# A kernel of attention, two mixing layers and a gated convolution: q of the first head pair in zero-padded tiles, first-layer copies a slot later in the drain, a block's split moved into the value layer

## The chip, the cores and the metric

One core of a Trainium2 chip runs the whole program. The metric is the device time of one execution in microseconds; several executions are timed and their median is given. The engines are named PE (TensorE), DVE (VectorE), ACT (ScalarE), POOL (GpSimd) and SP (SyncE). Each takes its instructions in the order in which the program issues them; DMAs are issued from the queues of SP, ACT and POOL.

## The reference, cut to what matters

All inputs are float32 except the weights, which come as float64: batch 4, 8 heads, 576 rows, head size 64, so a model width of 512.

```python
scores = q @ k.T / sqrt(64)                       # per batch and head, 576 x 576
scores = where(scores >= max(scores) - tau, scores, -1e9)
attn = exp(scores - max(scores)); attn /= sum(attn) + 1e-9
x = attn @ v                                      # heads side by side: 4 x 576 x 512
u = x + (x.T @ U @ V).T                           # rank 32, over the rows
y = u + relu(u @ w_ch1) @ w_ch2                   # 512 -> 2048 -> 512
gate = sigmoid(sum(conv_w[k] * y shifted by 4 - k rows, k = 0..4))
out = (gate * (y @ w_val)) @ w_out
```

## The kernel before, in words

Every product of float32 matrices is done with numbers split in two: a high part, rounded by a copy to the fast matmul type, and a low part, the rest (number minus high part). A product is then three matmuls (high by high, high by low, low by high), four for the scores of pair 0. The high part is nearly always a copy on ACT, the low part a subtraction on DVE behind it.

**Attention** goes through 16 pairs of heads, nine tiles of 128 query rows for each pair. Each tile is a slot `s`: nine slots a pair, `NS` = 155 slots with the drain. A slot takes one tile through one step of each stage: `scores` on PE, `soft_max` (L412, DVE: negation and maximum), `soft_exp` (L426, exponential on ACT, and L427, the threshold `th` on POOL, which the mask needs), `soft_mask` (L437, DVE), transposes `trans_main` and `trans_tail` (L453, L470), then `pv` (L496, L507), `back`, `mix_t`, `mix_u` and `mix_ut` for the whole pair. The copies that follow a PE step are put down with `later(s + 1, k, fn, name)`: they are issued in slot `s + 1` in four batches `k`, each sorted by `LATE_ORDER`. PE's steps of a slot come after them, sorted by `ORDER`.

q and k of a pair are loaded by `load_qk` (L258, DMAs at L266 and L271), transposed by `prep_T` (L327, L335, L338) and split by `hi_lo_qk` (L306; L313 and L315 on ACT, L319 and L323 on DVE). From pair 1 on, `stacks` copies high and low parts with DMAs into tiles `st` of 128 rows, in which high and low part lie one above the other. Pair 0 has no stacks: `scores` takes 64 rows of `qk` for each head (L386, L398, and L391 where the columns are rotated). Tile 0 of each pair takes the last 64 rows of both heads from `bd`, which `tails` (L369, four POOL copies) fills. Setup order is L571 to L616; `warm` is a series of transposes of the identity, and the four batches of copies of pair 0 are issued behind it.

Loads of weights and their conversion from float64 (`from_f64`, L103 to L131) are generators that `work.tick()` moves on a step at a time.

**The drain.** From slot 144 on, no scores are left, and each slot also takes one step of `dense_front` (L780): it splits block 0 of u (512 columns; `split_block`, L749 on ACT, L750 on DVE), runs the first layer `h1` (L767) on blocks 0 and 1, one tile of 12 matmuls (`passes`, L765) and its two copies (L773, L774) a slot, and splits blocks 1 and 2.

**The dense layers** run over four chunks of the hidden width and five blocks of columns (four of 512, one of 256): `h1` and `ch` (L818, L826) in turn, so that one tile's copies lie beside the next one's matmuls. Behind them come the gates (`gate_step`: taps on ACT, L834; L849 on DVE; sigmoid, L841), the value layer `val` (L885: 12 matmuls, product with the gate L895 on DVE, high part L896 on ACT, low part L897 on DVE) and `proj` (L903, L911), whose tiles ACT copies (L915) and SP stores (L917). `val` of block n + 1 needs the split of y's block n + 1, which stood behind `val` of block n.

Of the kernel before, what the change touches and what calls it, by code (L numbers as in the profile page):

```python
# [36 lines left out]
def attention_moe_kernel(  # L37
# [188 lines left out]
    def attention(dense_front, dense_mid, dense_back):  # L226
# [31 lines left out]
        def load_qk(p):  # L258
            eng = nc.gpsimd if 1 < p < 4 else nc.sync
            b, h = divmod(2 * p, H)  # L260
# [3 lines left out]
            for nm, src, o in (("qn", q, "(t p) d -> p t d"), ("kn", k, "(p t) d -> p t d")):  # L264
                for hh in range(2):
                    eng.dma_start(  # L266
                        out=t[nm][:, :, hh * D:(hh + 1) * D], in_=src[b, h + hh, 0:SM, :].rearrange(o, p=128)
                    )
                    yield
# [56 lines left out]

        def prep_T(s, p, nm):  # L327
            d = st8[p]
            if nm == "q":
                d["qk"] = qk_p.tile([128, 4, S], F32R, tag="qk", name="qk")  # L330
            x = xtile("tm")
            parts = []
            if nm != "tail":
                for i in range(4):
                    nc.tensor.transpose(x[:, i * 128:(i + 1) * 128], d[nm + "n"][:, i, :], idn)  # L335
                parts.append(hi_lo_qk(p, nm, x, 0, SM))
            else:
                nc.tensor.transpose(x[:, 0:128], d.pop("tn"), idn)  # L338
                for m, nn in enumerate("qk"):
                    parts.append(hi_lo_qk(p, nn, x[:, m * TL:(m + 1) * TL], SM, TL))  # L340
# [31 lines left out]
        def scores(p, i):  # L372
# [5 lines left out]
            else:  # L378
# [6 lines left out]
                else:  # L385
                    z = d["qk"][hh * D:(hh + 1) * D]  # L386
                    ops = [(z[:, m, c:c + 128], z[:, n, :]) for m in (0, 3) for n in (1, 2)]
# [30 lines left out]
        def soft_exp(p, i):  # L418
# [8 lines left out]
            nc.gpsimd.tensor_tensor(out=th, in0=nm, in1=tau_eff, op=ALU.add)  # L427
# [142 lines left out]

        for p in range(2):  # L571
            for _ in load_qk(p):
                pass
        nc.scalar.dma_start(out=tau_sb, in_=tau.partition_broadcast(128))
        make_identity(nc, idn)
        nc.scalar.activation(out=ntau, in_=idn[:, 0:1], func=ACTF.Exp)
# [32 lines left out]
        for nm in ("q", "k", "tail"):  # L609
# [5 lines left out]
        tails(0)  # L615
# [52 lines left out]
        for s in range(NS):  # L668
# [39 lines left out]
            if s >= 9 * NP:  # L708
                next(dense_front, None)
                for _ in range(1): work.tick()  # L710
# [34 lines left out]
    def split_block(src, pool=None):  # L745
        t = (pool or p1["us"]).tile([128, 2, KD, NB], F32R, tag="us", name="us")
        for o, m, s in src:
            for e in range(0, KD, 2):
                nc.scalar.activation(out=t[:, 0, e:e + 2, o:o + m], in_=s[:, e:e + 2], func=ACTF.Copy)  # L749
                nc.vector.tensor_tensor(  # L750
                    out=t[:, 1, e:e + 2, o:o + m], in0=s[:, e:e + 2], in1=f(t[:, 0, e:e + 2, o:o + m]),
                    op=ALU.subtract,
                )
        return t
# [12 lines left out]
    def h1(c, us, n):  # L767
        m = size[n]
        t = p1["h"].tile([128, 2, KD, NB], F32R, tag="h", name="h")
        for e in range(KD):  # L770
            ps = p1["a"].tile([128, 512], F32, tag="a", name="a")
            passes(ps, w1[c % 2][0], us, e, m)
            nc.scalar.activation(out=t[:, 0, e, 0:m], in_=ps[:, 0:m], func=ACTF.Relu)  # L773
# [3 lines left out]
            yield t  # L777


    def dense_front():  # L780
# [4 lines left out]
        us = split_block(u_src(0), p1["us"])  # L785
        yield
# [3 lines left out]
        for t in h1(0, us, 0):  # L790
# [4 lines left out]
        for t in h1(0, us2, 1):  # L795
            yield
        p1["t"].append(t)
        yield
# [15 lines left out]
    def dense():  # L814
# [70 lines left out]
        def val(n, ys):  # L885
            t = p1["h"].tile([128, 2, KD, NB], F32R, tag="h", name="g")
            for e in range(KD):
# [4 lines left out]
                m = size[n]  # L892
                passes(ps, w1[NCH % 2][0], ys, e, m)
                g = u[:, e, n * NB:n * NB + m]
                nc.vector.tensor_tensor(out=g, in0=ps[:, 0:m], in1=g, op=ALU.mult)  # L895
                nc.scalar.activation(out=t[:, 0, e, 0:m], in_=g, func=ACTF.Copy)  # L896
                nc.vector.tensor_tensor(out=t[:, 1, e, 0:m], in0=g, in1=f(t[:, 0, e, 0:m]), op=ALU.subtract)  # L897
                tick()
            return t
# [3 lines left out]
        def proj(n, t):  # L903
            w = w2[NCH % 2][0]
            for g in range(size[n] // 128):
# [9 lines left out]
                nc.scalar.activation(out=o, in_=ps, func=ACTF.Copy)  # L915
                r0 = n * NB + g * 128
                nc.sync.dma_start(out=outf[r0:r0 + 128, :], in_=o)  # L917
# [30 lines left out]
        for n in range(NN):  # L948
            t = val(n, us)
            if n + 1 < NN:  # L950
                us = split_block(y_src(n + 1))
# [40 lines left out]
```

## Time and profile before

| | |
|---|---|
| median of 3 runs | 856.49 us |
| the runs | 854.17, 859.28, 856.49 us |
| the profiled execution's own time | 854.32 us |
| its span | 852.4 us |
| mean granted clock of PE | 0.994 |
| PE busy | 826.8 us, 97% of the span |
| DVE, ACT, POOL busy | 609.9, 438.2, 241.5 us |

The profiled execution is one more run than the three. Its span goes from the first to the last thing the profiler saw; 1.9 us of its time lie outside. A busy PE is not PE at its peak, since matmuls overlap; so the places where it waits and the clock that it was granted are read beside the share. The granted clock of 1.00 is 2.4 GHz, 0.50 is 1.2 GHz. In a timeline row, the bracket gives the idle time of the engine before the instruction and what ended it.

### The profile page before, as it was taken

Reading aid. Unit: us, or ns where it says so; the run is one execution under the profiler, and the core shown is the slowest. Engines: PE = TensorE matmul, PEld = TensorE weight load, DVE = VectorE, ACT = ScalarE, POOL = GpSimd, SP = SyncE. Lnnn points to the kernel's source line nnn. Section 1 sums busy time; section 2 is a strip of 40 time slices with the busy share of each in tenths; the row PEclk is TensorE's granted clock in tenths of the full one; section 3 lists DMA queues with packets and bytes.
Section 4 is the critical chain, followed back from the end, with each engine's and each line's share of the span. In section 5 each row is a group of like instructions: output and inputs, shape, how many; then the busy total and the mean of one; then the engine's idle time right before and its main releaser. Section 6 shows DMA issues by size and latency. Waiting matters only on the chain.

```text
span 852.4 us, 14266 instructions
## 1 busy us (share of the span) xinstructions
PE 826.8 (97%) x5084; PEld 695.1 (82%) x5084; DVE 609.9 (72%) x1293; ACT 438.2 (51%) x890; POOL 241.5 (28%) x342
## 2 busy tenths in 40 slices
PE   8999999999999999899999999999999999999998
PEld 7887887887887888678888888888888888878886
DVE  6689888888988987436784785347753588988850
ACT  4688888887887887422232333133322334345532
POOL 6756433632433422001341244003420143200000
PEclk9799999999999999999999999999999999999999
DMA  5665755765675541001220122002210111001111
GB/s 133 159 142 127 175 134 129 167 160 129 149 174 129 133 107 46 0 1 50 75 74 26 49 75 75 1 1 77 71 50 1 41 58 50 1 1 38 62 50 75
DMA packets 63423, 68.07 MB, mean 80 GB/s; under 512 B 43333, under 2 KB 46549, under 8 KB 63354
## 3 DMA queue, kind: packets, MB, share of 16 engines
q1 hardware_dynamic: 61786, 64.07, 29.3%
q0 software_dynamic: 1424, 3.10, 1.3%
q8 instruction: 41, 0.67, 0.3%
q14 instruction: 28, 0.23, 0.1%
q10 hardware_dynamic: 144, 0.00, 0.0%
HBM read 35.89 MB, written 4.72 MB: 48 GB/s over the span
## 4 chain that ended last, share of the span: by engine, by line
PE 75%; DVE 10%; ACT 6%; issue 2%; DMA 2%; POOL 2%; SPq 1%; ACTq 0%; POOLq 0%; DVEq 0%
PE a L765 23%; PE c L765 20%; PE o L507 7%; PE p L911 6%; PE s L398 5%; PE v L765 5%; PE xm L453 4%; DVE u L849 3%; PE t L546 2%; PE o L496 2%; DVE e L437 1%; ACT pt L462 1%; DMA qn<-in_q_dram 1%; ACT e L426 1%; ACT qk L313 1%
## 5 line engine op out<-in xcount | busy, mean ns | idle before, releaser
L765 PE MATMUL c<-h,w 128*128 128x512 f32 (+1 forms) x960 | 200.9, 368 | 1.3 <-ACT u L568 1.3
L765 PE MATMUL a<-us,w 128*128 128x512 f32 (+1 forms) x960 | 201.5, 368 | 0.0
L765 PEld LDWEIGHTS c<-h,w 128*128 128x128 f32 x960 | 167.3, 189 | 31.7 <-ACT u L568 1.7
L765 PEld LDWEIGHTS a<-us,w 128*128 128x128 f32 x960 | 167.2, 189 | 30.2 <-issue 0.4
L773 ACT ACTIVATE h<-a 128x512 fp32r<-128x512 f32 (+1 forms) x80 | 44.2, 554 | 196.9 <-PE a L765 196.7
L427 POOL TENSOR_TENSOR th<-nm,tau_eff 128x1 f32<-128x1 f32 x144 | 81.5, 566 | 182.7 <-DVE ns L412 181.2
L131 POOL TENSOR_TENSOR wf<-wf,wt 128x512 f32<-128x512 f32 (+2 forms) x43 | 57.2, 1330 | 257.2 <-DVE wt L126 257.2
L774 DVE SCALAR_TENSOR_TENSOR h<-a,h 128x512 fp32r<-128x512 f32 (+1 forms) x80 | 50.9, 637 | 108.1 <-ACT h L773 107.9
L412 DVE TENSOR_SCALAR_CACHE_REDUCE ns<-s 128x576 f32<-128x576 f32 x144 | 108.3, 752 | 26.3 <-PE s L398 25.8
L437 DVE SCALAR_TENSOR_TENSOR e<-ns,th,e 128x576 f32<-128x576 f32 x144 | 119.6, 831 | 6.7 <-POOL th L427 6.3
L426 ACT ACTIVATE e<-ns,nm 128x576 f32<-128x576 f32 x144 | 111.4, 773 | 23.1 <-DVE ns L412 22.7
L398 PE MATMUL s<-st 128*128 128x288 f32 x480 | 94.7, 319 | 2.6 <-DVE ns L412 2.4
L453 PE MATMUL xm<-idn,e 128*128 128x128 f32 x576 | 88.8, 278 | 7.2 <-DVE qk L323 6.0
L462 ACT ACTIVATE pt<-xm 128x512 f32<-128x512 f32 x144 | 85.1, 591 | 4.9 <-PE xm L453 2.4
L398 PEld LDWEIGHTS s<-st 128*128 128x128 f32 x480 | 68.2, 189 | 16.6 <-issue 7.7
L453 PEld LDWEIGHTS xm<-idn,e 128*128 128x128 f32 x576 | 69.8, 142 | 12.8 <-ACT pt L462 6.0
L507 PE MATMUL o<-pt,vt 128*64 128x256 f32 (+1 forms) x768 | 69.8, 331 | 0.0
L507 PEld LDWEIGHTS o<-pt,vt 128*64 128x64 f32 x768 | 41.4, 137 | 24.5 <-issue 8.0
L172 POOL TENSOR_TENSOR w<-wf,w 128x512 fp32r<-128x512 f32 x36 | 54.0, 1516 | 10.0 <-ACT w L170 10.0
L849 DVE SCALAR_TENSOR_TENSOR u<-y,cw,u 128x576 f32<-128x576 f32 x64 | 55.0, 873 | 0.6
L826 DVE TENSOR_TENSOR y<-c,y 128x64 f32<-128x64 f32 (+4 forms) x96 | 39.8, 448 | 21.2 <-PE c L765 21.2
L750 DVE TENSOR_TENSOR us<-u,us 128x1024 fp32r<-128x1024 f32 (+1 forms) x40 | 46.8, 1211 | 10.2 <-ACT us L749 10.1
(108 smaller groups left out, 1034.1 us busy)
## 6 DMA issues: line engine op xcount, KB each, us to landing
raw<-in_moe_w_ch_dram SPq DMA_DIRECT2D x32, 512.0 KB, 4.0
st<-qk SPq DMA_DIRECT2D x30, 256.0 KB, 3.9
st<-qk SPq DMA_DIRECT2D x15, 432.0 KB, 3.9
st<-qk SPq DMA_DIRECT2D x45, 144.0 KB, 4.4
out_dram<-ring SPq DMA_DIRECT2D x18, 256.0 KB, 2.0
st<-qk SPq DMA_DIRECT2D x15, 288.0 KB, 4.9
qn<-in_q_dram SPq DMA_DIRECT2D x28, 128.0 KB, 3.5
kn<-in_k_dram SPq DMA_DIRECT2D x28, 128.0 KB, 3.4
```

Source lines behind the costliest of these rows:

```text
L131: nc.gpsimd.tensor_tensor(out=dst, in0=dst, in1=tf, op=ALU.add)
L172: lo_eng.tensor_tensor(out=lo, in0=w, in1=f(hi), op=ALU.subtract)
L398: nc.tensor.matmul(s[:, n, 0:HS], lhs, rhs[:, n * HS:(n + 1) * HS], start=(m == 0), stop=(m == len(ops) - 1))
L412: nc.vector.tensor_scalar(out=ns.rearrange("p (a b) -> p a b", a=2), in0=s, scalar1=-1.0, scalar2=3.0e38, op0=ALU.mult, op1=ALU.min, accum ...
L426: nc.scalar.activation(out=row(p, i), in_=d["ns", i], func=ACTF.Exp, bias=nm[:, 0:1], scale=-1.0)
L427: nc.gpsimd.tensor_tensor(out=th, in0=nm, in1=tau_eff, op=ALU.add)
L437: nc.vector.scalar_tensor_tensor(out=e, in0=d.pop(("ns", i)), scalar=d.pop(("th", i))[:, 0:1], in1=e, op0=ALU.is_le, op1=ALU.mult, accum_o ...
L453: nc.tensor.transpose(x[:, j * 128:(j + 1) * 128], e[:, c + j * 128:c + (j + 1) * 128], idn)
L462: later(s + 1, 0, lambda: nc.scalar.activation(out=dst, in_=x.rearrange("p (j c) -> p j c", j=4), func=ACTF.Copy), "x")
L507: nc.tensor.matmul(o, lhs, rhs, start=False, stop=stop)
L765: nc.tensor.matmul(ps[:, 0:m1], lhs, rhs, start=(m == 0), stop=(m == len(ops) - 1))
L849: nc.vector.scalar_tensor_tensor(out=g, in0=y[:, e, b, k:k + S], scalar=cw[:, k, e:e + 1], in1=g, op0=ALU.mult, op1=ALU.add)
```

## The change

Pair 0: q is loaded from ACT's queue; k, the tails and q are prepared in this order; each head's high and low part of q goes into a tile of 128 rows whose other 64 are filled with zeros, and the tails go into `bd` straight from PSUM, on ACT and DVE, without POOL. The scores of pair 0 use these tiles. The thresholds of pair 0 are computed on DVE. Drain: block 0 is split in quarters, the last three of them in the following slot; the two copies of a first-layer tile are issued a slot later; block 2 is split a slot sooner. Value layer: the low part of a tile is issued one tile later, the next block's split ahead of the last tile's product. End: the last output tile is copied and stored in halves.

```diff
         def load_qk(p):
             eng = nc.gpsimd if 1 < p < 4 else nc.sync
+            q_eng = eng if p else nc.scalar
...
-                    eng.dma_start(
+                    (q_eng if nm == "qn" else eng).dma_start(
...
+        def hi_lo_q0(hh, dst, ps):
+            a = slice(hh * D, (hh + 1) * D)
+            hi, lo = dst[0][a], dst[1][a]
+            return (
+                lambda: nc.scalar.activation(out=hi, in_=ps[a], func=ACTF.Copy, scale=qscale[a, 0:1]),
+                lambda: nc.vector.scalar_tensor_tensor(
+                    out=lo, in0=ps[a], scalar=qscale[a, 0:1], in1=f(hi), op0=ALU.mult, op1=ALU.subtract
+                ),
+            )
+
         def prep_T(s, p, nm):
...
-                parts.append(hi_lo_qk(p, nm, x, 0, SM))
+                if nm == "q" and not p:
+                    for hh in range(2):
+                        t = d["st", hh]
+                        parts.append(hi_lo_q0(hh, (t[:, 0, 0:SM], t[:, 1, 0:SM]), x))
+                else:
+                    parts.append(hi_lo_qk(p, nm, x, 0, SM))
+            elif not p:
+                nc.tensor.transpose(x[:, 0:128], d.pop("tn"), idn)
+                parts.append(hi_lo_qk(p, "k", x[:, TL:2 * TL], SM, TL))
+                for hh in range(2):
+                    o = slice(hh * D, (hh + 1) * D)
+                    parts.append(hi_lo_q0(hh, (bd[0][:, 0, o], bd[0][:, 1, o]), x[:, 0:TL]))
...
-                    z = d["qk"][hh * D:(hh + 1) * D]
-                    ops = [(z[:, m, c:c + 128], z[:, n, :]) for m in (0, 3) for n in (1, 2)]
+                    ops = [(d["st", hh][:, m, c:c + 128], d["qk"][:, n, :]) for m in (0, 1) for n in (1, 2)]
...
-            nc.gpsimd.tensor_tensor(out=th, in0=nm, in1=tau_eff, op=ALU.add)
+            (nc.gpsimd if p else nc.vector).tensor_tensor(out=th, in0=nm, in1=tau_eff, op=ALU.add)
...
+        nc.scalar.dma_start(out=tau_sb, in_=tau.partition_broadcast(128))
         for p in range(2):
             for _ in load_qk(p):
                 pass
-        nc.scalar.dma_start(out=tau_sb, in_=tau.partition_broadcast(128))
         make_identity(nc, idn)
+        for hh in range(2):
+            t = st8[0]["st", hh] = st_p.tile([128, 3, S], F32R, tag="st", name="st")
+            nc.vector.memset(f(t[(1 - hh) * D:(2 - hh) * D, 0:2, 0:SM]), 0.0)
...
-        for nm in ("q", "k", "tail"):
+        for nm in ("k", "tail", "q"):
             prep_T(-3, 0, nm)
...
-        tails(0)
...
             if s >= 9 * NP:
-                next(dense_front, None)
-                for _ in range(1): work.tick()
+                steps = next(dense_front, None)
+                if s == 9 * NP:
+                    later(s + 1, 0, lambda: list(steps))
+                work.tick()
...
-    def split_block(src, pool=None):
+    def split_steps(src, pool=None, k=2):
...
-            for e in range(0, KD, 2):
-                nc.scalar.activation(out=t[:, 0, e:e + 2, o:o + m], in_=s[:, e:e + 2], func=ACTF.Copy)
+            for e in range(0, KD, k):
+                nc.scalar.activation(out=t[:, 0, e:e + k, o:o + m], in_=s[:, e:e + k], func=ACTF.Copy)
...
+                yield t
+
+    def split_block(src, pool=None):
+        for t in split_steps(src, pool):
+            pass
         return t
...
-    def h1(c, us, n):
+    def h1(c, us, n, apart=False):
...
             passes(ps, w1[c % 2][0], us, e, m)
+            if apart:
+                yield t
             nc.scalar.activation(out=t[:, 0, e, 0:m], in_=ps[:, 0:m], func=ACTF.Relu)
...
-            yield t
+            if not apart:
+                yield t
...
     def dense_front():
...
-        us = split_block(u_src(0), p1["us"])
-        yield
+        steps = split_steps(u_src(0), p1["us"], 1)
+        us = next(steps)
+        yield steps
...
-        for t in h1(0, us, 0):
+        for t in h1(0, us, 0, True):
...
-        for t in h1(0, us2, 1):
+        for t in h1(0, us2, 1, True):
             yield
         p1["t"].append(t)
-        yield
         p1["s"] = split_block(u_src(2), p1["us"])
...
         def val(n, ys):
...
+            m, nxt = size[n], None
+
+            def low_part(e):
+                g = u[:, e, n * NB:n * NB + m]
+                nc.vector.tensor_tensor(out=t[:, 1, e, 0:m], in0=g, in1=f(t[:, 0, e, 0:m]), op=ALU.subtract)
...
                 passes(ps, w1[NCH % 2][0], ys, e, m)
+                if e == KD - 1 and n + 1 < NN:
+                    nxt = split_block(y_src(n + 1))
                 g = u[:, e, n * NB:n * NB + m]
                 nc.vector.tensor_tensor(out=g, in0=ps[:, 0:m], in1=g, op=ALU.mult)
                 nc.scalar.activation(out=t[:, 0, e, 0:m], in_=g, func=ACTF.Copy)
-                nc.vector.tensor_tensor(out=t[:, 1, e, 0:m], in0=g, in1=f(t[:, 0, e, 0:m]), op=ALU.subtract)
+                if e:
+                    low_part(e - 1)
                 tick()
-            return t
+            low_part(KD - 1)
+            return t, nxt
...
-                nc.scalar.activation(out=o, in_=ps, func=ACTF.Copy)
                 r0 = n * NB + g * 128
-                nc.sync.dma_start(out=outf[r0:r0 + 128, :], in_=o)
+                if r0 + 128 < T:
+                    nc.scalar.activation(out=o, in_=ps, func=ACTF.Copy)
+                    nc.sync.dma_start(out=outf[r0:r0 + 128, :], in_=o)
+                else:
+                    hc = DM // 2
+                    nc.scalar.activation(out=o[:, 0:hc], in_=ps[:, 0:hc], func=ACTF.Copy)
+                    nc.vector.tensor_copy(out=o[:, hc:DM], in_=ps[:, hc:DM])
+                    nc.scalar.dma_start(out=outf[r0:r0 + 128, 0:hc], in_=o[:, 0:hc])
+                    nc.sync.dma_start(out=outf[r0:r0 + 128, hc:DM], in_=o[:, hc:DM])
...
-            t = val(n, us)
-            if n + 1 < NN:
-                us = split_block(y_src(n + 1))
+            t, us = val(n, us)
```

## Rows read from the trace of the kernel before

**Rows 1.** The page's chain of waits: share of the span by engine.

```profile
PE 75%; DVE 10%; ACT 6%; issue 2%; DMA 2%; POOL 2%; SPq 1%; ACTq 0%; POOLq 0%; DVEq 0%
```

**Rows 2.** Windows: stretch, length, busy PE, PEld, DVE, ACT, POOL, clock, DMA share, GB/s.

```profile
9.00:22.90 13.90, 12.92 (x89) 10.89 (x89) 11.98 (x33) 7.53 (x15) 9.99 (x20) 1.00 0.44 112
22.90:33.10 10.20, 10.20 (x41) 8.49 (x40) 4.52 (x11) 5.49 (x11) 9.50 (x17) 0.50 0.99 248
```

**Rows 3.** The chain of waits, pair 0: start us, us, what.

```profile
12.23 1.62 PE s L391 x12
...
14.43 1.26 PE s L398 x8
...
15.69 0.60 PE xm L453 x4
...
34.49 0.66 PE o L496 x4
...
35.15 2.34 PE o L507 x32
...
37.49 0.73 PE s L398 x4
```

**Rows 4.** Timeline of PE, pair 0: start us, us, engine, line, output<-inputs, count, [idle before].

```profile
21.47 1.76 PE L391 MATMUL s<-qk 64*128 64x64 f32 x12 [0.84 <-DVE ns L412]
...
23.17 1.11 PE L453 MATMUL xm<-idn,e 128*128 128x128 f32 x4
...
31.41 1.79 PE L398 MATMUL s<-qk,bd 128*128 128x288 f32 x6
```

**Rows 5.** Timeline of VectorE, pair 0.

```profile
27.51 1.58 DVE L437 SCALAR_TENSOR_TENSOR e<-ns,th,e 128x576 f32<-128x576 f32 x1 [2.62 <-POOL th L427]
...
32.84 0.82 DVE L437 SCALAR_TENSOR_TENSOR e<-ns,th,e 128x576 f32<-128x576 f32 x1 [3.06 <-POOL th L427]
...
36.53 0.17 DVE L443 TENSOR_SCALAR sum<-sum 128x9 f32<-128x9 f32 x1
```

**Rows 6.** Timeline of all engines, the start.

```profile
0.74 1.00 SPq L266 DMA_DIRECT2D qn<-in_q_dram  x2
...
3.70 0.55 DVE L603 MEMSET bd<- 128x256 f32 x2
...
6.20 0.69 ACT L313 ACTIVATE qk<-tm,qscale 128x512 fp32r<-128x512 f32 x1 [3.50 <-PE tm L335]
...
7.15 0.30 PE L338 MATMUL tm<-idn,tn 128*128 128x128 f32 x1 [0.55 <-DMA tn<-in_k_dram]
...
8.54 0.86 POOL L369 TENSOR_SCALAR bd<-qk 64x64 fp32r<-64x64 f32 x3 [0.41 <-DVE qk L319]
...
9.14 1.25 PE L398 MATMUL s<-qk,bd 128*128 128x288 f32 x6 [0.16 <-POOL bd L369]
```

**Rows 7.** Timeline of all engines, the drain of attention.

```profile
340.66 2.00 ACT L749 ACTIVATE us<-u 128x1024 fp32r<-128x1024 f32 x2 [0.50 <-issue]
...
343.20 0.33 PE L470 MATMUL xk<-idn,e 128*128 128x128 f32 x1 [1.58 <-ACT pt L462]
...
362.29 1.38 PE L546 MATMUL t<-ring,u 128*128 128x128 f32 x10 [2.01 <-DVE ring L532]
...
374.07 11.22 PE L765 MATMUL c<-h,w 128*128 128x512 f32 x48 [1.29 <-ACT u L568]
```

**Rows 8.** Timeline of all engines, the first blocks of the value layer.

```profile
752.55 5.91 PE L765 MATMUL c<-h,w 128*128 128x256 f32 x48
...
757.96 2.18 ACT L749 ACTIVATE us<-y 128x128 fp32r<-128x128 f32 x4
...
759.35 0.49 PE L765 MATMUL v<-us,w 128*128 128x512 f32 x1 [0.89 <-ACT us L749]
...
760.97 10.95 PE L765 MATMUL v<-us,w 128*128 128x512 f32 x47 [1.12 <-DVE us L750]
```

**Rows 9.** Timeline of all engines, the last copy of the kernel.

```profile
848.50 0.60 ACT L915 ACTIVATE ring<-p 128x512 f32<-128x512 f32 x1 [2.12 <-PE p L911]
```

## What the change does to the time: the prediction

> **What bounds the kernel now.** I read the chain of waits first. PE holds three quarters of it [rows 1]: what PE does without a pause cannot get shorter by moving copies about, so the change can only win where PE idles, where PE runs at the lower of its two clocks, or after PE's last matmul. The waits of PE and the windows then give three such places.
>
> The first is pair 0. From 22.9 to 33.1 us the granted clock is 0.50, 1.2 GHz in place of 2.4; PE is busy all 10.20 us of it [rows 2]. Before the fall PE had run score tiles whose operands fill 64 of the 128 rows, with one pause of 0.84 us at 21.47; the clock came back while the first tile of pair 1 ran, the first since the start whose operands fill 128 rows [rows 4]. In the same stretch VectorE twice stood still for a threshold from POOL, 2.62 and 3.06 us [rows 5]. PE was busy through both, so these waits alone cost little: the slow PE is the bound and the thresholds sit just under it.
>
> The second is the drain of attention, where PE waits 1.58, 2.01 and 1.29 us [rows 7]; the third is the value layer's second block, which waits 0.89 and 1.12 us for its split [rows 8].
>
> **The change part by part. Pair 0, the clock.** Padding each head's q with zeros makes the tiles 128 rows deep. Depth costs no PE time: eight 64-row matmuls take 1.26 us, four 128-row ones 0.73 [rows 3], so about 0.16 and 0.18 each. The work from the transposes at 23.17 to the value matmuls at 35.15 lasted 11.98 us. At the full clock it is four groups of transposes (4 x 0.60), scores of 1.26 and 1.62, the six matmuls of pair 1's first tile (1.25 by pair 0's [rows 6]) and 0.66 for the tails' matmuls, with 0.2 for two small transposes: 7.4 us [rows 3]. Gain 4.6. What lies beside it must keep up: the masks no longer wait for POOL, since the thresholds move to VectorE. If the clock stays up and the thresholds had stayed on POOL, those two waits would be next in line.
>
> The Trainium skill ("SBUF — State Buffer", "Who interferes with whom") says that a VectorE instruction with two SBUF inputs contends with a GpSimd instruction that reads SBUF. The mask is one, and the trace agrees: 1.58 us beside POOL's work, 0.82 at 32.84 [rows 5]. By that rule POOL, freed of its thresholds, runs beside the masks: 0.76 us on three of them would take 2.3 us from the gain if none of it were covered. I take none off: at the full clock a mask is needed about every 2 us (a score tile and its transposes) and VectorE's two passes of 0.8 leave room.
>
> **Pair 0, the thresholds.** Nine 128x1 additions go into VectorE's queue, right behind the reduction that makes their input. The nearest row is a 128x9 add at 0.17 us [rows 5]; none shows this form on VectorE, so each costs between nothing and 0.2 with its issue. VectorE is busy 11.98 of 13.90 us up to 22.9 [rows 2], so seven of them, 0 to 1.4 us, delay what follows; I take 0.13 each, 0.9 us.
>
> **Pair 0, the start.** Removed: POOL's four copies, of which three stood between q's tail and the first scores (8.54 to 9.40, scores at 9.14) [rows 6]. q's two loads go to ScalarE's queue (two took 1.00 us of issue on SP); what they push back there is covered by the 3.50 us for which ScalarE waited before its first copy at 6.20, and without that cover would come 1.0 us later. SP reaches k, then the tails, 1.0 us sooner, so the tail's transpose, which waited for its load until 7.15, runs at about 6.2. Added: q's copies in two halves per step; I price a half like the whole (ScalarE 0.69 [rows 6]; VectorE 0.73, the mask's 0.82 for 576 columns [rows 5] taken down to 512), the lower bound being half of it. The new order puts k, tails, then q on both engines: first scores at about 8.3, but VectorE still has q's two low parts before its first reduction, at about 9.7 in place of 10.4. Gain 0.7, and at least 0. The two zero fills on VectorE are 8 times one fill of 256 columns (0.55 for two), so 2.2 us; they run at the start, where VectorE has only three small operations on tau ahead of that row at 3.70, and would delay the start one for one if they had no such cover. Start and thresholds cancel: 0.7 against 0.9; I count the pair as 0, with bounds of -1.4 and +0.7. **Pair 0 in all: 4.6.** If the 0.84 pause goes too, it is 5.4.
>
> **The drain.** The split of block 0 ran as two copies of 1.00 us ahead of the copy for which PE's transpose waited [rows 7]. Now a first copy of a quarter stands there, and three follow behind that copy: 1.5 us are out of the way, and PE waits 0.1 in place of 1.58. Next late is the low part of the last quarter, needed for the last three of the first tile's twelve matmuls; three copies of 0.5 and a subtraction of 0.7 are done 2.2 us after the copy, as PE comes there (nine matmuls of 0.23, by the 48 in 11.22 [rows 7]). Gain 1.4. The second wait, 2.01, is a transposed product that waits for a scaling on VectorE; in front of that stood ScalarE's copy of a first-layer tile, itself waiting for PE's twelve matmuls. Issued a slot later, that copy stands behind the scaling: gain 2.0. The third, 1.29, is the copy of u queued behind the last first-layer tile; again it now goes first: gain 1.3. What is queued behind a late copy is only its low part and the buffer (four, and a fifth tile comes a slot after the copy). Split of block 1 now runs before the first tile's copy, which PE doesn't need until 374. **Drain: 4.7**, bounds 2.0 (the scaling alone) and 4.9.
>
> **The value layer.** PE's matmuls of the other layer end at 752.55 + 5.91 = 758.46; the split's copies started at 757.96, since they stood behind the last product's chain, with VectorE 4 us behind PE [rows 8]. Now the split stands before that product, and its copies can start once PE has left the block, at 752.5. Four copies of 2.18 in all and the last subtraction, 0.7, put it at 755.4, and what VectorE still has ahead of it at about 756. PE goes on at 758.46: gain 0.89 + 1.12 = 2.0. The last product's low part comes later by the split (about 2.5 us), but it feeds a projection that stands 11 us behind on PE. The low parts, one step late, no longer make VectorE wait for ScalarE.
>
> **The end.** The last tile's copy, 0.60 us [rows 9], becomes two of half the width on two engines, each with its own store. Half of 0.60 is the upper bound; I take 0.2, with nothing for the store.
>
> Sum: 4.6 + 4.7 + 2.0 + 0.2 = 11.5 us. The profiled execution took 854.3, so 842.8 by its own measure. It lies 2.2 below the median of the three runs, 856.5; I add a third of this, as a choice, and predict 843.5.
>
> **The rivals.** (a) The clock falls all the same: the cause is the pause of 0.84 us, or the zeros don't count, and the padding doesn't do what it is made for. For it: the pause comes 1.4 us before the fall and VectorE's queue, which causes it, only gets longer. Against it: the clock stays low for 10.2 us in which PE never pauses [rows 2], and returns at the first 128-row tile. PE is then the bound as before, pair 0 gains nothing, and the time is 854.3 - 6.9 = 847.4. Chance 0.13.
>
> The Trainium skill ("TensorE: Matmul & The Clock Gate", "HAM oscillation — how this bites in real kernels") puts the fall of the clock down to pauses of PE, which is (a). The trace agrees only in that a pause came first; 10.2 us of busy PE at 0.50 speak against it as the whole cause.
>
> (b) VectorE becomes pair 0's bound: nine thresholds at 0.2 and one more low part of 0.73 for q are 2.5 us, on an engine that is busy 86% before 22.9 [rows 2]. The clock holds, pair 0 gains 2.1, the time is 845.3. Chance 0.11.
>
> (c) Slower: in the new form the half-empty tiles count for less than before, and the clock is low from the first scores on. At half clock a group of transposes takes 1.11 us in place of 0.60, so PE's 12.92 us up to 22.9 [rows 2] grow by 0.85 of themselves, 11.0 us: 854.3 + 11.0 - 6.9 = 858.4. It decides from about 15 us more of low clock than now, since each loses 0.46. Speaks against it: the same 64 rows of data held the clock for 13.9 us. Chance 0.04.
>
> **How the numbers follow.** The forecast keeps 0.72. A measurement of this kernel can tell 0.5%, 4.3 us, from no change; the forecast, (a) and (b) lie below 852.2, (c) nearly all above 856.5. Faster 0.95, same 0.02, slower 0.03. Low end: 0.8 for the pause, 0.7 for the start, 0.5 for drain, value layer and end, and something for the offset: 840.0. High end: (a) with the whole offset to the median, 849.6.
>
> **What would show it.** Granted clock 1.00 from 20 to 35 us and no wait of VectorE on POOL there; value matmuls of pair 0 near 30.5 in place of 35.15; in the drain none of the three waits over 0.3; the value layer's second block following the other layer without a gap. A clock of 0.50 in pair 0 refutes the first step; waits of PE on the first-layer copies, or on VectorE in the value layer, the others.

## The result, and the profile after

| | before | after |
|---|---|---|
| median | 857.35 us (4 executions, 854.17 to 859.28) | 842.65 us (4 executions, 841.62 to 843.46) |
| ratio, 95% interval | | 0.9827 (0.9801 to 0.9853) |
| the profiled execution's own time, its span | 854.32, 852.4 us | 843.46, 841.5 us |
| mean granted clock in it | 0.994 | 0.997 |

The change makes the kernel faster by 1.7%; the forecast was 843.5 us, in a range of 840.0 to 849.6. From one profiled execution to the other it is 10.9 us, against a forecast of 11.5. Where the 10.9 us came from is read off by comparing the same instruction in both traces; the difference between two places is the gain of the stretch between them.

| place | before | after | gained so far | in this stretch | forecast |
|---|---|---|---|---|---|
| pair 0's first value matmuls | 35.08 | 31.87 | 3.2 | pair 0: 3.2 | 4.6 |
| second layer's first matmul | 374.07 [rows 7] | 366.00 | 8.1 | drain: 4.8 | 4.7 |
| value layer's second block, second matmul | 760.97 [rows 8] | 750.06 + 0.23 | 10.7 | value: 2.4 | 2.0 |
| last copy | 848.50 [rows 9] | 837.71 | 10.8 | | |
| end of the span | 852.4 | 841.5 | 10.9 | end: 0.1 | 0.2 |

All are timeline rows; that of the first place before is

```profile
35.08 2.41 PE L507 MATMUL o<-pt,vt 128*64 128x64 f32 x32
```

and the chain's 35.15 [rows 3] stands against 31.94 in the chain of the changed kernel, 3.2 as well. 0.23 us is one matmul, so that the second one is compared with the second. Not counted in a stretch are small drifts between the places: 0.1 up to the drain (the last pair's value matmuls start at 337.31 and 334.02), 0.2 from its end to the other layer's matmuls, which start at 752.55 [rows 8] and 744.30, and 0.1 in the last 88 us.

The chain of waits on the page of the changed kernel:

```profile
PE 82%; DVE 6%; ACT 5%; issue 2%; DMA 2%; POOL 1%; SPq 0%; ACTq 0%; DVEq 0%; POOLq 0%
```

PE's share has gone from 75% to 82% [rows 1]: what was taken out were steps of other engines, and PE's own at half clock. The windows of pair 0, the two of [rows 2] and then three of 3 us (columns as in [rows 2]):

```profile
9.00:22.90 13.90, 11.09 (x83) 9.84 (x82) 13.32 (x38) 7.51 (x16) 6.04 (x9) 1.00 0.34 91
22.90:33.10 10.20, 9.79 (x80) 9.02 (x81) 9.45 (x29) 7.02 (x16) 9.74 (x14) 0.83 0.99 236
21.00:24.00 3.00, 1.89 (x14) 1.45 (x12) 2.97 (x7) 1.81 (x4) 2.58 (x3) 1.00 0.72 147
24.00:27.00 3.00, 2.74 (x12) 2.77 (x13) 2.93 (x11) 2.04 (x4) 2.71 (x7) 0.55 0.94 226
27.00:30.00 3.00, 3.00 (x24) 2.98 (x24) 2.42 (x8) 1.72 (x5) 2.88 (x3) 0.88 1.05 221
```

The clock still falls, but for 3.4 us in place of 10.2 (twice what is missing to 1.00: 0.45 and 0.12 of 3 us each). And VectorE is now busy 13.32 of the 13.90 us up to 22.9, where it was 11.98: PE works 11.09 of them and waits for the rest. The waits of PE in the first 40 us say for what:

```profile
PE s L420 <- DVE ns L434: 1.3, 1, 1.3
PE s L413 <- DVE ns L434: 1.1, 2, 1.0
PE xm L475 <- DVE e L459: 0.7, 2, 0.4
```

The timeline of PE shows where they lie and what follows:

```profile
18.80 1.33 PE L420 MATMUL s<-qk,st 128*128 128x288 f32 x8 [1.34 <-DVE ns L434]
...
22.16 1.69 PE L413 MATMUL s<-qk,st 128*128 128x64 f32 x12 [0.96 <-DVE ns L434]
24.26 1.05 PE L475 MATMUL xm<-idn,e 128*128 128x128 f32 x4 [0.41 <-DVE e L459]
24.96 2.27 PE L420 MATMUL s<-qk,st 128*128 128x288 f32 x8
...
27.84 1.67 PE L413 MATMUL s<-qk,st 128*128 128x64 f32 x12
...
31.87 1.98 PE L529 MATMUL o<-pt,vt 128*64 128x64 f32 x28
```

Eight score matmuls take 1.33 us at 18.80 and 2.27 at 24.96, behind three pauses that sum to 2.7 us; at 27.84 the full rate is back, while pair 0's own padded tiles run. Before, the rate came back only at pair 1's tile [rows 4].

The timeline of VectorE, start and middle of pair 0:

```profile
9.02 1.53 DVE L334 SCALAR_TENSOR_TENSOR st<-tm,qscale,st 64x512 fp32r<-64x512 f32 x2 [0.70 <-ACT st L333]
10.59 0.76 DVE L434 TENSOR_SCALAR_CACHE_REDUCE ns<-s 128x576 f32<-128x576 f32 x1
...
11.39 0.16 DVE L449 TENSOR_TENSOR th<-nm,tau_eff 128x1 f32<-128x1 f32 x1
...
22.14 0.47 DVE L449 TENSOR_TENSOR th<-nm,tau_eff 128x1 f32<-128x1 f32 x1
...
22.83 1.27 DVE L459 SCALAR_TENSOR_TENSOR e<-ns,th,e 128x576 f32<-128x576 f32 x1
```

q's two low parts, 1.53 us, stand ahead of the first reduction, which starts at 10.59: the start has gained nothing there. Before, it was

```profile
10.43 0.76 DVE L412 TENSOR_SCALAR_CACHE_REDUCE ns<-s 128x576 f32<-128x576 f32 x1 [1.84 <-PE s L398]
```

A threshold takes 0.16 us, 0.47 at worst.

The drain, on PE; of its three waits [rows 7] only 0.21 us of the first are left:

```profile
338.53 0.33 PE L492 MATMUL xk<-idn,e 128*128 128x128 f32 x1 [0.21 <-ACT pt L484]
...
355.74 1.27 PE L568 MATMUL t<-ring,u 128*128 128x128 f32 x10
...
366.00 1.30 PE L796 MATMUL c<-h,w 128*128 128x512 f32 x5
```

The value layer's first two blocks, PE and ScalarE: the split now runs from 745.30, a microsecond into the other layer's matmuls, and PE goes on at 750.06 with no idle time in brackets, where it waited twice [rows 8]:

```profile
744.30 5.92 PE L796 MATMUL c<-h,w 128*128 128x256 f32 x48
...
745.30 2.18 ACT L775 ACTIVATE us<-y 128x128 fp32r<-128x128 f32 x4
...
750.06 2.23 PE L796 MATMUL v<-us,w 128*128 128x512 f32 x9
```

The last copy. Its halves don't run side by side: VectorE's begins 0.42 us after ScalarE's, and ends at 838.55, 0.84 us after the first began; the whole copy took 0.60 [rows 9]. So the copy itself got slower.

```profile
837.71 0.38 ACT L965 ACTIVATE ring<-p 128x256 f32<-128x256 f32 x1 [2.12 <-PE p L955]
...
838.13 0.42 DVE L966 COPY ring<-p 128x256 f32<-128x256 f32 x1 [15.48 <-ACT ring L965]
```

### The profile page after: what moved, and what is told of

The parts are those of the page before. It is cut to its first block, busy times and chain, and to the rows that moved or that the text cites. A ratio compares the mean times of both kernels' runs of the same rounds, so it can differ in the third digit from the quotient of the medians.

```text
span 841.5 us, 14257 instructions
## 1 busy us (share of the span) xinstructions
PE 821.6 (98%) x5084; PEld 693.7 (82%) x5084; DVE 613.7 (73%) x1309; ACT 439.3 (52%) x894; POOL 238.3 (28%) x329
## 4 chain that ended last, share of the span: by engine, by line
PE 82%; DVE 6%; ACT 5%; issue 2%; DMA 2%; POOL 1%; SPq 0%; ACTq 0%; DVEq 0%; POOLq 0%
PE a L796 24%; PE c L796 23%; PE o L529 7%; PE v L796 6%; PE p L955 6%; PE s L420 5%; PE xm L475 4%; PE t L568 2%; DVE e L459 2%; PE o L518 2%; DVE ns L434 2%; DMA qn<-in_q_dram 1%; ACT qk L314 1%; DVE qk L324 1%; ACT e L448 1%
## 5 line engine op out<-in xcount | busy, mean ns | idle before, releaser
L796 PEld LDWEIGHTS a<-us,w 128*128 128x128 f32 x960 | 167.2, 189 | 30.5 <-DVE us L776 0.4
L449 POOL TENSOR_TENSOR th<-nm,tau_eff 128x1 f32<-128x1 f32 x135 | 78.2, 580 | 177.2 <-DVE ns L434 175.7
```

What stands on the lines that cost most here:

```text
L449: (nc.gpsimd if p else nc.vector).tensor_tensor(out=th, in0=nm, in1=tau_eff, op=ALU.add)
L796: nc.tensor.matmul(ps[:, 0:m1], lhs, rhs, start=(m == 0), stop=(m == len(ops) - 1))
```

## The experiments

All kernels compute the whole reference. They start from the changed kernel, and a diff shows what they take back or add. Three groups were run, each on one chip with its own executions of the kernel before: the first four (median before 856.71 us), the next four (857.71) and the last four (859.27). Intervals are of the ratio to those.

**Thresholds of pair 0 back on POOL, the padding kept** (e1_th_pool).

```diff
-            (nc.gpsimd if p else nc.vector).tensor_tensor(out=th, in0=nm, in1=tau_eff, op=ALU.add)
+            nc.gpsimd.tensor_tensor(out=th, in0=nm, in1=tau_eff, op=ALU.add)
```

> The changed kernel with the thresholds of pair 0 back on POOL; padding kept. Theory 1 (the padding alone holds the clock, PE bounds pair 0): value matmuls of pair 0 start within 0.7 us of the changed kernel's 31.94, time within 1 us of its 842.7. Theory 2 (the queues behind the thresholds bound it): VectorE waits again 2 to 3 us, once or twice, for POOL, PE pauses with it, the clock falls for longer than 3.5 us, value matmuls at 34.5 or later, time 845 to 847.

848.99 us, ratio 0.9912 (0.9882 to 0.9943): 6.3 above the changed kernel, and 2 above the range expected for the second theory. Value matmuls of pair 0 start at 36.64, later than before the change (35.08). Waits of PE, then of VectorE, in the first 40 us, and two windows:

```profile
PE xm L475 <- DVE e L459: 4.7, 2, 2.5
...
DVE e L459 <- POOL th L449: 3.1, 1, 3.1
...
27.00:30.00 3.00, 0.50 (x5) 0.42 (x4) 2.11 (x3) 1.04 (x3) 2.79 (x4) 1.00 1.02 214
...
33.00:36.00 3.00, 1.90 (x8) 1.89 (x9) 2.78 (x7) 1.25 (x3) 1.75 (x4) 0.50 0.42 128
```

The clock holds until 30 us. PE gets faster, and runs into the masks that wait for POOL: it works 0.50 of 3.00 us, and only then does the clock fall. (The page shows one of VectorE's two waits for POOL, 3.1 us. The other, 2.6 us, it puts down to a copy of ScalarE; POOL's threshold ends at 27.85, and the mask starts at 27.89.) The two waits of [rows 5] were free as long as PE was slow, and become the bound when it isn't. So padding alone gains nothing in this profile.

**Tiles of 64 rows as before, with their loads, order and POOL copies; thresholds on VectorE** (e2_rows64).

```diff
-        for nm in ("k", "tail", "q"):
+        for nm in ("q", "k", "tail"):
             prep_T(-3, 0, nm)
...
-                    ops = [(d["st", hh][:, m, c:c + 128], d["qk"][:, n, :]) for m in (0, 1) for n in (1, 2)]
+                    z = d["qk"][hh * D:(hh + 1) * D]
+                    ops = [(z[:, m, c:c + 128], z[:, n, :]) for m in (0, 3) for n in (1, 2)]
...
```

> The changed kernel with pair 0's q as before (64-row tiles, old loads, old order, tails through POOL); thresholds stay on VectorE. If the rows hold the clock: granted clock 0.50 for some 8 to 10 us before 33, value matmuls of pair 0 at 34.5 or later, time 845 to 846.5. If the thresholds gave the gain: clock low for at most 4 us, value matmuls near 32, time near 842.7.

847.66 us, 0.9897 (0.986 to 0.9934), 1.2 above the range expected; value matmuls at 36.34. Windows:

```profile
21.00:24.00 3.00, 2.04 (x10) 2.02 (x10) 2.97 (x9) 1.81 (x4) 2.69 (x3) 0.61 0.77 157
24.00:27.00 3.00, 3.00 (x13) 2.39 (x12) 2.93 (x10) 1.96 (x4) 2.71 (x7) 0.50 0.97 231
...
30.00:33.00 3.00, 3.00 (x14) 2.72 (x14) 0.96 (x3) 0.78 (x2) 2.75 (x4) 0.50 0.96 292
```

The clock falls behind the same kind of pause (1.0 us) and stays at 0.50 from 24 to 33 with PE busy throughout; in the changed kernel, after longer pauses, it was back in 3.4 us. The thresholds alone gain nothing either. Neither half of the change in pair 0 has a gain of its own in its profile (36.64 and 36.34 against 35.08); together they reach 31.87.

**Weight conversions spread** (e5_spread): the loaders take one step a slot in slots 2 to 7, not two, so that VectorE has less to do there.

```diff
-                if at == 3 and (s < 18 or s % 18 in CONVERT_AT) or at == 1 and 2 <= s < 8:
+                if at == 3 and (s < 18 or s % 18 in CONVERT_AT):
```

> The changed kernel with one conversion step a slot in place of two in slots 2 to 7, so that U's and V's conversions spread over more slots. Theory 1 (VectorE's full queue bounds pair 0 of the changed kernel and its pauses of PE let the clock fall): PE's waits on VectorE between 15 and 25 us, 2.7 us now, drop under 1 us, no stretch of low clock, value matmuls of pair 0 at 30.5 or sooner, time 840.5 to 841.7. Theory 2 (the work only moves into pair 1): value matmuls of pair 1 not before 50.5 (50.79 now), time 842 to 843.

842.25 us, 0.9833 (0.9803 to 0.9863). Value matmuls at 30.71, clock 1.00 in every window of pair 0, and mean clocks of 0.999 to 1.0 in its four executions. Pair 1's value matmuls start at 49.57 (50.72 in the changed kernel), so the work did not just move there. PE still waits, 1.6 + 1.0 + 0.8 us, but in six pieces of at most 0.9, and VectorE is still busy 2.93 to 2.97 of every 3 us up to 33. The spread took no load off the bound, only the longest pause, and with it the fall. The median gains 0.4 on the changed kernel, less than the intervals tell apart.

**The same with 64 rows** (e6_rows64_spread): the edit of e2_rows64, and on it

```diff
-                if at == 3 and (s < 18 or s % 18 in CONVERT_AT) or at == 1 and 2 <= s < 8:
+                if at == 3 and (s < 18 or s % 18 in CONVERT_AT):
```

> 64-row tiles and thresholds on VectorE as in the run before, and the conversions spread. If PE's pauses alone make the clock fall: with fewer pauses it stays at 1.00 in spite of the 64 rows, value matmuls of pair 0 at 31 or sooner. If the rows matter by themselves: the clock falls between 15 and 30 us with PE busy, and stays low until pair 1's first tile; value matmuls at 33.5 or later, time 844.5 to 846.

842.89 us, 0.984 (0.981 to 0.9871), between the two expectations; value matmuls at 31.81; mean clock 1.0 in two of its four executions. Timeline of PE in the profiled one, and two windows of 2 us:

```profile
25.69 1.69 PE L402 MATMUL s<-qk 64*128 64x64 f32 x12 [0.37 <-DVE ns L423]
...
24.00:26.00 2.00, 1.63 (x13) 1.23 (x11) 1.97 (x7) 0.86 (x3) 1.07 (x1) 1.00 0.81 216
...
28.00:30.00 2.00, 1.73 (x8) 1.45 (x7) 1.97 (x7) 1.53 (x3) 0.73 (x2) 0.50 1.14 237
```

Here 64-row tiles run at the full clock up to 27 us, behind pauses of 0.2 to 0.4 us. So 64 rows don't by themselves bring the clock down; ahead of the two long falls with PE busy (the kernel before, e2_rows64) there was a pause of 0.84 and 1.0 us, and 64-row tiles followed in both. Here the fall came late, and pair 1's first tile, at 28.59, was near. With the spread, padding is worth 0.6 us (842.89 against 842.25), without it 5.0 (847.66 against 842.65): thresholds on VectorE and a spread of its conversions would have done nearly as much without padding.

**Drain as before** (e3_drain_old): whole split at once, first-layer copies in their own slot, block 2 split a slot later.

```diff
-        steps = split_steps(u_src(0), p1["us"], 1)
-        us = next(steps)
-        yield steps
+        us = split_block(u_src(0), p1["us"])
+        yield
...
-        for t in h1(0, us, 0, True):
+        for t in h1(0, us, 0):
...
```

> The changed kernel with the drain as before. If the drain's three waits are what its part of the change is worth: the second layer's first tile starts 4.6 to 5.0 us later than in the changed kernel (against the start of the last pair's value matmuls), PE waits 1.6, 2.0 and 1.3 us there, time 847 to 848. If the time would have been given back later: under 2 us, 843 to 844.6.

847.43 us, 0.9877 (0.9851 to 0.9902): 4.8 above the changed kernel's first median. The three waits are back, with the old sizes:

```profile
PE t L568 <- DVE ring L554: 2.0, 1, 2.0
PE xk L492 <- ACT pt L484: 1.6, 1, 1.6
PE c L794 <- ACT u L590: 1.3, 1, 1.3
```

**Value layer as before** (e4_val_old): split behind the block, low parts at once.

```diff
-                if e == KD - 1 and n + 1 < NN:
-                    nxt = split_block(y_src(n + 1))
...
-                if e:
-                    low_part(e - 1)
+                low_part(e)
...
-            low_part(KD - 1)
+            if n + 1 < NN:
+                nxt = split_block(y_src(n + 1))
```

> The changed kernel with the split behind the value layer's block and the low parts at once. If the split alone stood in the way: a gap of about 2.5 us before the second block, time 845 to 845.5. If other waits of that stage take its place: under 1 us, 843 to 843.6.

845.58 us, 0.9853 (0.9823 to 0.9883): 2.9 above. The waits of PE from 690 us on are those of [rows 8]:

```profile
PE v L796 <- DVE us L776: 1.1, 1, 1.1
PE v L796 <- ACT us L775: 0.9, 1, 0.9
```

These prices let the two halves of pair 0 be read by medians too. e1_th_pool lies 7.7 us below the kernel before of its group, e2_rows64 9.1; drain, value layer and end are worth about 7.8 of that (4.8, 2.9 and 0.1). What is left for pair 0 is -0.1 and 1.3, where the intervals reach 2.6 and 3.2 us to either side: no gain that can be told from nothing. For the whole change it is 14.7 less 7.8, or 6.9.

**Conversion of two weights off VectorE** (e7_uv_relief): a clamp goes to POOL, a scaling to ScalarE and POOL.

```diff
-            w = yield from convert(raw_uv[part])
+            w = yield from convert(raw_uv[part], 1, 1)
```

> The changed kernel with two steps of U's and V's conversions (clamp and low part's scaling, 1.75 us of VectorE) on POOL and ScalarE. If VectorE's queue bounds pair 0: PE's waits on VectorE between 15 and 25 us drop by half, value matmuls of pair 0 at 30 to 30.7 and no or a shorter stretch of low clock, time 841 to 842. If POOL's reads slow the masks as much as VectorE is relieved, or PE bounds: value matmuls after 31.2, time 842.3 to 843.3.

843.74 us, 0.9831 (0.9807 to 0.9856): no gain, and outside both of the expected ranges. VectorE is still busy 2.93 to 3.00 of 3 us from 18 to 24, PE's pauses are 1.6 + 1.2 + 0.9, the clock is 0.71 and 0.72 from 21 to 27. What was taken out of its queue did not open it: the conversion now runs through two more engines, and one mask waits 1.6 us for ScalarE.

**Both** (e8_spread_relief): the edits of e5_spread and e7_uv_relief.

```diff
-            w = yield from convert(raw_uv[part])
+            w = yield from convert(raw_uv[part], 1, 1)
...
-                if at == 3 and (s < 18 or s % 18 in CONVERT_AT) or at == 1 and 2 <= s < 8:
+                if at == 3 and (s < 18 or s % 18 in CONVERT_AT):
```

> Both: conversions spread and two of their steps off VectorE. If VectorE bounds pair 0: value matmuls of pair 0 at 29.0 to 30.2 in place of 30.78 with the spread alone, time 840 to 841.6. If the spread has taken all there is: at 30.6 to 31, time 842 to 842.5.

841.27 us, 0.9802 (0.9779 to 0.9826); value matmuls at 29.70, clock 1.00 throughout pair 0, PE's waits 1.0 + 0.8 + 0.6. It was run once more in the last group (e8b_again), beside the changed kernel (a2_changed).

> The changed kernel once more, beside the next run on one chip. Same time as before within 0.3%: 842 to 845. If the mean granted clock differs between its executions, the slower ones have the lower clock.

> Conversions spread and two of their steps off VectorE, once more. If VectorE's queue and the short stretch of low clock are what is left in pair 0 of the changed kernel: 1.5 to 3 us below the changed kernel on this chip, all executions at a clock of 0.999 or 1.0. If the difference came from the chips: within 0.7 us.

The changed kernel: 842.56 us (841.67 to 843.98), 0.9812 (0.9791 to 0.9833). Both: 841.12 us (840.88 to 841.49), 0.9795 (0.9776 to 0.9814). The intervals overlap; by medians the new version is 1.4 us better, just short of the 1.5 expected. On this chip the slowest of its five executions (841.49) lies below the fastest of the changed kernel's four (841.67); they lie within 0.6 us, those of the changed kernel within 2.3. Waits of PE up to 40 us, a window, and the value matmuls in the profiled execution of a2_changed, which is the changed kernel again:

```profile
PE s L420 <- DVE ns L434: 1.3, 1, 1.3
PE s L413 <- DVE ns L434: 1.1, 2, 1.0
PE xm L475 <- DVE e L459: 0.8, 2, 0.4
...
21.62 1.68 PE L413 MATMUL s<-qk,st 128*128 128x64 f32 x12 [0.96 <-DVE ns L434]
...
24.00:27.00 3.00, 3.00 (x26) 2.78 (x25) 2.93 (x11) 2.58 (x5) 2.71 (x7) 1.00 0.95 229
...
30.04 2.41 PE L529 MATMUL o<-pt,vt 128*64 128x64 f32 x32
```

The same pauses as in its first profile, and this time no fall: value matmuls at 30.04, 1.8 us sooner. Of this, 0.5 was there before any fall (21.62 against 22.16), since the first transposes ran faster; the fall cost 1.3. Its four executions line up by mean clock: 841.67 us at 1.0, 842.07 at 0.999, 843.05 at 0.998, 843.98 at 0.996. What is left to chance in the changed kernel is mainly whether its pauses lead to a fall.

Four more profiles have pair 0 as in the changed kernel, since their edits lie behind it: e3_drain_old, e4_val_old, e9_split_early and e10_quarters_only. All four show the same pauses (1.34, 0.33, 0.96 and 0.4; in e4_val_old not the last). Three keep the clock at 1.00, with value matmuls at 30.07 to 30.13. e4_val_old falls behind the pause of 0.96, and is back after 3.4 us:

```profile
21.00:24.00 3.00, 2.04 (x13) 1.87 (x12) 2.96 (x9) 1.82 (x4) 2.73 (x3) 0.82 0.78 158
24.00:27.00 3.00, 3.00 (x17) 2.94 (x17) 2.93 (x9) 2.22 (x4) 2.71 (x7) 0.61 0.95 228
```

So of six profiles of this pair 0, two show the fall and four don't, and the first profile is the unusual one. Each fall with padded tiles and no long pause inside (here, in the first profile and in e7_uv_relief) lasted 3.4 us; those of the kernel before and of e2_rows64 lasted 10.2 and, counted the same way (0.61 from 21 to 24 and from 33 to 36, 0.50 between), 13.7. And beside an execution without a fall the spread of e5_spread alone is no gain: its value matmuls come at 30.71, 0.7 later than here, 0.4 of which is a later start (first reduction at 10.48 against 10.06).

**Value layer: split early, low parts at once** (e9_split_early).

```diff
-                if e:
-                    low_part(e - 1)
+                low_part(e)
...
-            low_part(KD - 1)
```

> The changed kernel with the low parts of the value layer issued at once again, the split still ahead of the last product. If the split alone gives that stage's gain: no gap before the second block, time as the changed kernel's within 0.5 us. If the late low parts are needed too, since VectorE's waits of 0.76 us for ScalarE delay the split: a gap of 0.5 to 2 us.

842.42 us, 0.9811 (0.979 to 0.9831), and PE has no wait from 690 us on. The place of the split is all of the gain; the late low parts give nothing that can be measured.

**Drain: quarters kept, first-layer copies at once, block 2 split a slot later** (e10_quarters_only).

```diff
-        for t in h1(0, us, 0, True):
+        for t in h1(0, us, 0):
...
-        for t in h1(0, us2, 1, True):
+        for t in h1(0, us2, 1):
...
+        yield
```

> The changed kernel with the drain's first-layer copies issued at once again, block 0 still split in quarters. If the drain's three waits are independent: PE waits 2.0 and 1.3 us there and not 1.6, time 3.2 to 3.6 us above the changed kernel. If the waits shift into one another: less than 2 or more than 4.5 us above it.

847.13 us, 0.9862 (0.9842 to 0.9881): 4.6 above a2_changed, more than the two waits that were to return. That is the range expected for waits that shift into one another, but the waits came back with their old sizes, and the rest is the clock. Timeline of PE in the drain, and a window:

```profile
356.24 2.50 PE L568 MATMUL t<-ring,u 128*128 128x128 f32 x10 [2.01 <-DVE ring L554]
358.39 6.27 PE L796 MATMUL a<-us,w 128*128 128x512 f32 x24
...
369.61 2.57 PE L796 MATMUL c<-h,w 128*128 128x512 f32 x10 [1.29 <-ACT u L590]
...
356.20:358.40 2.20, 2.16 (x11) 2.16 (x11) 0.00 (x0) 0.00 (x0) 0.00 (x0) 0.50 0.03 7
```

Behind the wait of 2.01 us the clock fell to 0.50: the ten transposes take 2.50 us in place of 1.27, the 24 matmuls 6.27 in place of 5.74. That is 1.8, with the two waits 5.1 of the 5.3 us by which the second layer starts later relative to the value matmuls before the drain (332.30 to 369.61, in a2_changed 332.16 to 364.13). In e3_drain_old and in the kernel before (1.38 us for the ten [rows 7]) the same wait brought no fall in the profiled execution. The late copies are most of the drain's gain; the quarters keep the first wait at 0.2, and by medians can't be told from nothing (847.13 and 847.43, against different executions of before; e10_quarters_only carries the fall's 1.8, so the two are not like for like).

## Why the prediction was right

**Pair 0, the clock: right in kind, 4.6 for 3.2 measured, or 5.0.** The two numbers are two executions of one kernel, with the fall (31.87) and without (30.04); the forecast's 30.5 is near the second, and four of six profiles are like it. The step that failed is "VectorE's two passes of 0.8 leave room": with the thresholds, q's copies by halves and the weights' conversions VectorE's queue has next to no gap up to 27 us, and PE stops four times for it (1.34, 0.33, 0.96 and 0.41 us; before, up to 33 us, once, for 0.84 [rows 4]). The forecast is thus mixed with parts of rivals (a) and (b): the pause that goes ahead of the fall was not removed but multiplied, and VectorE is the bound of pair 0's first half.

The score matmuls behind the pause of 0.96 split pair 0 in two; before, they start at 21.47 [rows 4]. Up to there the change lost 0.7 us (22.16), or 0.2 (21.62 in a2_changed). From there to the value matmuls it was 13.6 us before, 9.7 with the fall and 8.4 without: a gain of 3.9 or 5.2. What the forecast had right, and (a) wrong, is that the clock is not low for 10.2 us any more: 3.4 us or none, with padded tiles. That padded rows shorten the fall is read from three falls against the two of the kernel before and e2_rows64; what it is in e2_rows64 (rows, order or loads) was not taken apart further, and by e6_rows64_spread the padding is not needed where PE's pauses are short.

The Trainium skill ("TensorE: Matmul & The Clock Gate", "HAM oscillation — how this bites in real kernels") puts falls down to PE's pauses. The falls behind 2.01 us in e10_quarters_only and behind 2.5 and 2.2 us in e1_th_pool agree in kind, though the Trainium skill's own case has longer pauses. The nine microseconds at 0.50 with PE busy 3.00 of 3.00 in e2_rows64 don't follow from it, nor does a2_changed staying at 1.00 behind 1.34 us, and the measurement decides: here a pause came ahead of each fall, but it settles neither whether the fall comes nor how long it lasts.

**Thresholds: near.** Forecast 0.13 each, seven of them ahead of 22.9 us; measured 0.16, and 0.19 of delay, for five: the read of the accumulator ahead of the first one starts at 11.27, the next reduction at 11.46, where an operation with no threshold before it starts together with that read (16.60). That is 1.0 us, or 1.3 with the one of 0.47, for the 0.9 forecast. And the conditional was right: had they stayed on POOL, the two waits would have been next in line. e1_th_pool prices that at 6.3 us, a number that the prediction had left out.

**Start: too high, 0.7 forecast, none measured, or 0.4.** First scores came at 8.66 in place of 9.14, but the first reduction at 10.59 (forecast about 9.7; before, 10.43), since q's two low parts stand right ahead of it. Their price was right (1.53 us for two, forecast 0.73 each, although each covers only 64 rows), but not their place: by the forecast they began at about 8.3, and they begin at 9.02, after 0.70 us of waiting for ScalarE's copy. In a2_changed, e3_drain_old, e9_split_early and e10_quarters_only the first transposes run faster (0.63 us for four in a2_changed, 1.06 in the first profile), and the first reduction starts at 10.06 to 10.10.

**Masks beside POOL.** One took 1.27 us at 22.83 against 0.82 for others. The Trainium skill ("SBUF — State Buffer", "Who interferes with whom") says that the mask, with two SBUF inputs, contends with GpSimd's reads; the trace agrees, with 0.45 us for this one. But not every mask beside POOL pays:

```profile
26.98 4.80 POOL L657 TENSOR_TENSOR vst<-wf,vst 32x352 fp32r<-32x352 f32 x4
28.18 0.81 DVE L459 SCALAR_TENSOR_TENSOR e<-ns,th,e 128x576 f32<-128x576 f32 x1
```

Before, the same four operations of POOL took 3.76 us, beside the mask of 1.58 [rows 5]; so here POOL may have paid, which no run took apart. The prediction took nothing off for the masks, since they were to have room; with VectorE's queue full, 0.45 counts.

**Drain: right,** 4.7 forecast, 4.8 measured, 4.8 by medians when taken back. **Value layer: right in place, 2.0 forecast, 2.4 measured** and 2.9 by medians when taken back; the gain is the earlier split alone. **End: 0.1 for 0.2,** and not by the step forecast: the copy was to get shorter and the store to count for nothing. VectorE's half starts only when ScalarE's is done, which the trace names as its releaser; why it has to, no run here shows. So the copy takes 0.84 us in place of 0.60, and what is gained lies behind it: a half's store takes 1.7 us from issue to landing, a whole one 2.0.

**The offset: the wrong sign.** A third of the way from the profiled execution to the median was added, 0.7 us. In the changed kernel the median lies 0.8 below the profiled execution (843.46), which was the slowest of the four. The kernel before shows mean clocks of 0.994 to 0.986 with times of 853.8 to 861.0 us, most of them in step; by the clock its time at 0.50 is 10 us in the profiled execution (0.006 of 854, doubled) and about twice that in others (0.988, 859 us). The change removes most of it, so the medians differ by 14.7 us where the profiled executions differ by 10.9. That the forecast comes within 0.9 us is partly luck: the sum for the profiled execution was 0.7 too low (842.8 for 843.46), most of all by pair 0, and the offset 1.5 too high.

## What to carry to other kernels

Where a slow PE covers waits of another engine, price both together: here the padding and the moved thresholds show no gain alone, and either one taken back costs 5 to 6 us. Put a small operation on the engine that makes its input when the other engine's queue is long, but look first at how full the receiving queue is; if it is full, spread what doesn't belong to this stretch (one line: the times then lie within 0.5 us in place of 2.3, and the padding is worth 0.6 us in place of 5.0). And where a kernel's executions differ, read the mean granted clock beside each time before taking the profiled one as typical.

## What the runs showed of the hardware that was not expected

- The same kernel with the same pauses (1.3, 1.0, 0.4 us) kept the clock at 1.00 in one execution and dropped to 0.50 for 3.4 us in another; of six profiles with this pair 0, four kept it.
- The same pause of 2.01 us in the drain was followed by 0.50 in e10_quarters_only and by 1.00 in the kernel before and in e3_drain_old.
- Tiles of 64 rows ran at 0.50 for nine microseconds of uninterrupted work in e2_rows64, and at 1.00 up to 27 us in e6_rows64_spread, where PE's pauses were at most 0.4 us from 18 us on.
- Two copies of halves of one PSUM tile on ScalarE and VectorE ran one after the other (0.38 and 0.42 us, 837.71 and 838.13) with both engines idle before. Whether it is the tile, the bank or the order of waits was not tried.
